# A two-layer network behind linear attention: where the weight products lie in SBUF, when chunk 2 does the next chunk's norm, and when raw weights are stored

## The chip, the cores and the metric

The kernel runs on one core of one Trainium2 chip. The metric is the device time of one execution in microseconds; lower is better. TensorE is called PE, its weight loads PEld, VectorE DVE, ScalarE ACT, GpSimd POOL and SyncE SP. SP issues all large DMAs, in order.

## The reference

```python
def _attn_ref(q, k, v, g_norm):                      # 8 batches, 8 heads, 576 tokens, 64 per head
    kv = np.einsum('bhsd,bhse->bhde', k, v)
    out = np.einsum('bhsd,bhde->bhse', q, kv)
    rms = np.sqrt(np.mean(out * out, axis=-1, keepdims=True) + 1e-06)
    return out / rms * g_norm
def _moe_ref(x, w_in, w_out):                        # x: 4608 x 512, w_in: 512 x 2048, w_out: 2048 x 512
    h = x @ w_in
    g = 0.5 * h * (1.0 + erf(h * np.float32(1.0 / np.sqrt(2.0))))
    return g @ w_out
```

`x` is the attention's output, one row of 512 for each of 4608 tokens. All is float32.

## The kernel before

**Tiling.** The tokens go in nine chunks `c` of 512. Each float32 operand of a large product is kept as two float32r parts, hi and lo, and a product is three matmuls: hi with hi, lo with hi, hi with lo. Chunks 0 and 1 multiply plainly, 16 blocks of the hidden layer one after the other, with matmuls 512 wide (`layer1`, L669, and `layer2`, L696), while the weights are converted and combined. From chunk 2 (`PLAIN`) on, the first layer takes seven products instead of eight for each 2 x 2 block of the matrices: a *pair* `j` (0 to 7) is two blocks of the hidden layer, its products `k` (0 to 6) are six matmuls 256 wide each (`product`, L537), 42 a pair. From chunk 3 (`FAST`) on the second layer does the same in 28 *ticks* `(k, n)` of twelve matmuls (`Fast.matmuls`, L1154). Chunk 2 is the bridge: pairs in the first layer, plain blocks in the second.

**Operands.** In `product` a combination of weights is the stationary operand and `x` the moving one; in `Fast.matmuls` the weights are moving and the activations stationary. The combined weights lie in DRAM (`products`), 512 KB for two of them, and are fetched by SP into a ring of six tiles (`RINGS`; `fetch`, L501): when the last matmul of a tile's content is issued, the content six places on is fetched. Four contents of the first layer stay in w_out4 to w_out7 (`KEPT_IN`, `keep`, L521), seven of the second in `KEPT_OUT`.

**Places.** A tile is 4096 bytes a partition, and the tiles lie in the order of `PLACES`, so all of them begin at the same residue modulo 256 bytes, but for what `EXTRA` adds. `LINE` is 16 floats, 64 bytes. A ring tile has 256 bytes more, in which a fetched content is moved on by `away`: 64 bytes for the first layer, 192 for the second. `KEPT_IN` lies 64 bytes on, `KEPT_OUT` 192 (w_out8 to w_out11, w_in13 to w_in15), and all behind them at residue 0 again. The tiles of `x` and of the activations lie at residue 0. The kv tiles of the attention lie 64 bytes below these, modulo 256. PE's order of matmuls comes from the program as written.

**The next chunk's attention in chunk 2.** Between the two halves of a pair's products, and behind it, `ahead`, `ahead_matmuls` and `ahead_loads` issue the work of chunk 3: `project` (PE, L243), `squares` (ACT, then a sum on DVE), `fold` (PE, L275), `rsqrt` (nine small operations on DVE, L290 to L308), `scale` (a transpose, L320, and a product, L316, on DVE for each of four parts), `add_blocks` (L357) and the split into hi and lo (ACT L362, DVE or POOL L367). `split_kv` (L193, L194) is for chunk 4.

**Weights of the second layer in chunk 2.** By the table `SUMS`, `sum_out` makes the sums of w_out's blocks on POOL (L528: two of 128 x 512, four of 128 x 256), `split_out` splits them on ACT and DVE (L1213, L1214), and `send` in the middle of the next pair has SP store them (L406). Names of buffers for this come from the list `free`. `raw_out` stores blocks that need no sum.

**What waits for what.** Every engine takes its instructions in the order written. A pair's copy on DVE (L553) reads the first product out of its PSUM bank; product 4 adds to that bank, so PE waits for the copy, and for all that stands ahead of it on DVE:

```python
        between[0]()
        product(at, j, 0, a[:, left], True)
        product(at, j, 1, a[:, right])
        nc.vector.tensor_copy(out=p1, in_=a[:, left])
        add(v, a[:, right], p1)
...
        product(at, j, 4, a[:, left])
```

Of the kernel before, what the change touches and what calls it, by code (L numbers as in the profile page):

```python
# [23 lines left out]
FAST = 3  # L24
# [13 lines left out]
def linear_attn_rms_gelu_ffn(  # L38
# [55 lines left out]
    IN_AWAY, OUT_AWAY = LINE, 3 * LINE  # L94
# [398 lines left out]
    def fetch(n):  # L493

        if n < len(queue):
            key = queue[n][1]
            i = RING[n % len(RING)]
            reused(i, F32R)
            away = IN_AWAY if key[0] == "in" else OUT_AWAY
            t = ring[n] = kept[i][:, away:away + 2 * DM]  # L500
            nc.sync.dma_start(out=t.bitcast(F32), in_=products[key])  # L501

    def operand(c, key):
        at = c, key
        return ring[place[at]] if at in place else resident[key]
# [24 lines left out]
    def product(at, j, k, out, first=False):  # L530
        *key, n = place_in(j, k)
        key = tuple(key)
        w, x = operand(at.c, key)[:, n * DM:(n + 1) * DM], at.x[k]
# [457 lines left out]
    def later(c, i):  # L991

        if i < NJ2 - 2:
            raw_out(i)
# [100 lines left out]
    class Fast:  # L1095
# [44 lines left out]
        def matmuls(self, i):  # L1140
# [7 lines left out]
            for p in range(2):  # L1148
                hi, lo = (op[:, z * CH + p * HALF:z * CH + (p + 1) * HALF] for z in range(2))
                wh, wl = (w[:, p * DM + m * HALF:p * DM + (m + 1) * HALF] for m in range(2))  # L1150
# [70 lines left out]
    def send():  # L1221

        for x in sent:
            if isinstance(x, str):
                free.append(x)
# [4 lines left out]
    def ahead(c, j, place):  # L1230
# [34 lines left out]
    def ahead_matmuls(c, j, between):  # L1265
        if c + 1 < NCH:
            for p in {(0, 0): (0,), (1, 0): (1,), (1, 1): (2,), (2, 0): (3,)}.get((j, between), ()):
                attn[c + 1].project(p)
            if (j, between) == (3, 0):
# [70 lines left out]
    SUMS = {0: (0,), 1: (1,), 2: (2, 3), 3: (4,), 4: (5, 6), 7: (7,)}  # L1340
    for c in range(PLAIN, FAST):
        for j in range(NJ2):
# [13 lines left out]
            for n in SUMS.get(j - 1, ()):  # L1356
                split_out(n)
# [98 lines left out]
```

## Time and profile before

| What | Value |
|---|---|
| median of 3 runs | 818.79 us (817.54 to 818.96) |
| the profiled execution | 817.35 us, span 815.5 us |
| PE, PEld busy | 797.0 us, 744.9 us |
| DVE, ACT, POOL busy | 566.2, 369.6, 202.9 us |
| mean granted PE clock | 0.994 |
| HBM read and written | 205.52 and 35.13 MB |

Chunks 0 and 1 end near 213 us, chunk 2 near 313, and a later chunk takes 78 to 90 us by the stages. In the timeline's rows a number ahead of an engine's name is a start and a length in us, `xN` stands for N instructions in a row, and brackets give the idle time of the engine before it and what ended it. A matmul's length overlaps that of the next, so the pace is read from start to start.

### The profile page before, as it was taken

The page shows a single profiled execution, that of the slowest core. Times are in us where ns is not written, and L with a number is a line of the kernel's source. Part 1 is how long each engine was busy: PE and PEld are TensorE (multiplying, and loading weights), DVE is VectorE, ACT ScalarE, POOL GpSimd, SP SyncE. Part 2 cuts the span into 40 slices and gives each one's busy share as a digit, 9 for nine tenths or more (in the row PEclk, how much of TensorE's full clock was granted, in tenths as well). Part 3 has the DMA queues.
Part 4 walks back from the last instruction along what each step waited for, and adds up shares of the span by engine and source line. Part 5 has one row for each costly group of instructions (what it writes and reads, how often), then busy time and mean ns, then how long its engine had stood idle before and what let it go on. Part 6 is the DMA issues. An engine that isn't in the chain of part 4 may idle for free.

```text
span 815.5 us, 16193 instructions
## 1 busy us (share of the span) xinstructions
PE 797.0 (98%) x6248; PEld 744.9 (91%) x6248; DVE 566.2 (69%) x1030; ACT 369.6 (45%) x702; POOL 202.9 (25%) x183
## 2 busy tenths in 40 slices
PE   8999999999997889999999999999999999999998
PEld 6688887888997779999999999999999999999998
DVE  3999756679457673779567865787479748965683
ACT  3788533434452242536254635353445443532361
POOL 1000021102349322380029002710163016201200
PEclk9999999999999799999999999999999999999999
DMA  9981328996797599999999998999889988999884
GB/s 352 409 348 52 117 64 285 362 334 222 295 364 238 196 364 335 393 376 338 348 313 354 326 357 303 361 304 315 307 310 319 324 307 306 291 326 340 315 303 162
DMA packets 90513, 245.39 MB, mean 301 GB/s; under 512 B 9029, under 2 KB 30789, under 8 KB 90437
## 3 DMA queue, kind: packets, MB, share of 16 engines
q1 hardware_dynamic: 90432, 244.35, 84.0%
q8 instruction: 50, 0.82, 0.4%
q14 instruction: 27, 0.21, 0.1%
q10 hardware_dynamic: 4, 0.00, 0.0%
HBM read 205.52 MB, written 35.13 MB: 295 GB/s over the span
## 4 chain that ended last, share of the span: by engine, by line
PE 92%; DMA 3%; DVE 3%; ACT 1%; issue 0%; DVEq 0%; SPq 0%; ACTq 0%
PE acc L1154 20%; PE acc L537 18%; PE h L537 14%; PE acc L696 14%; PE h L669 10%; PE a L1154 8%; PE a L243 3%; PE a L182 2%; DMA w_out<-kv_main 1%; PE h L661 1%; DMA products_out<-w_out 1%; DMA out<-z 1%; DVE w_out L1214 1%; DMA w_in<-products_in 1%; DVE t L299 0%
## 5 line engine op out<-in xcount | busy, mean ns | idle before, releaser
L696 PE MATMUL acc<-w_out,gh 128*128 128x512 f32 x312 | 97.5, 393 | 0.0
L669 PE MATMUL h<-x,w_in 128*128 128x512 f32 x360 | 87.4, 392 | 0.0
L230 POOL TENSOR_TENSOR ql<-q,qh 128x512 fp32r<-128x512 f32 x16 | 21.2, 1327 | 255.3 <-ACT qh L229 255.3
L1154 PE MATMUL acc<-w_in,w_out 128*128 128x256 f32 x660 | 82.7, 279 | 0.0
L669 PEld LDWEIGHTS h<-x,w_in 128*128 128x128 f32 x360 | 67.5, 188 | 14.6 <-POOL x L333 0.2
L1154 PEld LDWEIGHTS acc<-w_in,w_out 128*128 128x128 f32 x660 | 79.2, 188 | 0.0
L537 PE MATMUL acc<-w_out,w_in 128*128 128x256 f32 x540 | 74.4, 280 | 0.0
L696 PEld LDWEIGHTS acc<-w_out,gh 128*128 128x128 f32 x312 | 57.9, 188 | 12.2
L537 PEld LDWEIGHTS acc<-w_out,w_in 128*128 128x128 f32 x540 | 67.5, 188 | 0.3
L696 PE MATMUL acc<-w_out,gl 128*128 128x512 f32 x156 | 61.2, 393 | 1.8 <-DVE gl L688 1.8
L682 ACT ACTIVATE gh<-h 128x512 fp32r<-128x512 f32 x39 | 23.2, 595 | 75.0 <-PE h L669 55.2
L537 PE MATMUL h<-w_in,w_in 128*128 128x256 f32 x348 | 47.2, 287 | 9.7 <-DVE w_in L528 9.7
L537 PEld LDWEIGHTS h<-w_in,w_in 128*128 128x128 f32 x348 | 44.1, 196 | 10.3 <-DVE w_in L528 10.3
L537 PE MATMUL acc<-x,w_in 128*128 128x256 f32 x360 | 48.6, 280 | 0.0
L688 DVE TENSOR_TENSOR gl<-h,gh 128x512 fp32r<-128x512 f32 x39 | 26.8, 686 | 28.9 <-ACT h L683 24.4
L1154 PE MATMUL acc<-w_in,x 128*128 128x256 f32 x360 | 45.8, 279 | 0.0
L537 PEld LDWEIGHTS acc<-x,w_in 128*128 128x128 f32 x360 | 44.7, 188 | 0.3
L537 PE MATMUL h<-w_out,w_in 128*128 128x256 f32 x324 | 44.6, 279 | 0.0
L1154 PEld LDWEIGHTS acc<-w_in,x 128*128 128x128 f32 x360 | 43.5, 188 | 0.0
L537 PE MATMUL h<-x,w_in 128*128 128x256 f32 x312 | 41.6, 280 | 0.5 <-PE acc L696 0.5
L528 DVE TENSOR_TENSOR gl<-acc,gh 128x256 f32<-128x256 f32 (+1 forms) x66 | 29.2, 442 | 18.3 <-ACT gh L574 14.6
L537 PEld LDWEIGHTS h<-w_out,w_in 128*128 128x128 f32 x324 | 40.7, 189 | 0.1
(288 smaller groups left out, 1800.3 us busy)
## 6 DMA issues: line engine op xcount, KB each, us to landing
w_in<-products_in SPq DMA_DIRECT2D x172, 512.0 KB, 5.3
w_in<-products_out SPq DMA_DIRECT2D x126, 512.0 KB, 5.2
kv_main<-kv_main SPq DMA_DIRECT2D x22, 512.0 KB, 6.1
products_in<-w_in SPq DMA_DIRECT2D x40, 256.0 KB, 4.9
w_in<-w_in SPq DMA_DIRECT2D x16, 512.0 KB, 10.2
w_out<-w_out SPq DMA_DIRECT2D x16, 512.0 KB, 10.0
q<-qT SPq DMA_DIRECT2D x15, 512.0 KB, 6.7
products_out<-w_out SPq DMA_DIRECT2D x30, 256.0 KB, 5.3
```

The lines of the kernel that those rows point to most:

```text
L182: nc.tensor.matmul(out=ps[r, n * D:(n + 1) * D], lhsT=k[:, r], rhs=v[:, r], start=(j == 0), stop=(j == NJ),)
L230: eng.tensor_tensor(out=ql, in0=q, in1=qh.bitcast(F32), op=ALU.subtract)
L243: nc.tensor.matmul(out=ps[:, a:e], lhsT=w, rhs=x[:, a:e], start=(m == 0), stop=(m == 2))
L528: eng.tensor_tensor(out=out, in0=x, in1=y, op=op)
L537: nc.tensor.matmul(out=out, lhsT=y, rhs=x[:, z, kb], start=first and kb + i == 0, stop=kb == 1 and i == 2, skip_group_check=True,)
L661: nc.tensor.matmul(out=h, lhsT=ws[i].bitcast(F32)[:, p * P:(p + 1) * P], rhs=at.o_all[:, p], start=(p == 0), stop=(p == NP - 1),)
L669: nc.tensor.matmul(out=h, lhsT=parts["in", i][:, w][:, p * P:(p + 1) * P], rhs=at.x[p][:, x], start=(m + p == 0), stop=(m == 2 and p == NP ...
L682: nc.scalar.activation(out=gh, in_=h, func=AF.Gelu)
L688: nc.vector.tensor_tensor(out=gl, in0=h, in1=gh.bitcast(F32), op=ALU.subtract)
L696: nc.tensor.matmul(out=ps, lhsT=x[:, ts], rhs=parts["out", i][:, w], start=(i == 0 and m == 0), stop=(m == 2 and (i == NF - 1 or (i, t) == ...
L1154: nc.tensor.matmul(out=ps[:, a * HALF:(a + 1) * HALF], lhsT=x[:, at], rhs=y, start=(k in (0, 2, 1) and n + p + a + m == 0), stop=(n == GRO ...
L1214: nc.vector.tensor_tensor(out=t[:, :, 1], in0=s[:, h], in1=t[:, :, 0].bitcast(F32), op=ALU.subtract)
```

## The change

It has four parts. (1) Places: contents of the first layer are moved on by 192 bytes like those of the second, but the first content of each pair has its first product at 0 and its second at 192, in two DMAs of 256 KB instead of one of 512; the second layer's first content (tick 0) lies at 0. `KEPT_IN` is now 192 bytes on. (2) Chunk 2: projections, squares, fold, `rsqrt` and scaling each come one slot sooner, the first scaling's product on POOL. (3) `SUMS` takes one sum behind each of pairs 0 to 3 and 5, two behind pair 4; sum 5's halves go to w_out4 and w_out5, so that w_out6 and w_out7 are loaded first by `keep`. (4) `raw_out` runs two slots later in chunk 1, and its last two calls move from the start of chunk 3 into pairs 1 and 3.

```diff
-    IN_AWAY, OUT_AWAY = LINE, 3 * LINE
+    AWAY = 3 * LINE
...
-    EXTRA[RINGS[-1]] += IN_AWAY
-    EXTRA[KEPT_IN[-1]] = OUT_AWAY - IN_AWAY
-    EXTRA[KEPT_OUT[-1]] = 4 * LINE - OUT_AWAY
+    EXTRA[RINGS[-1]] += AWAY
+    EXTRA[KEPT_OUT[-1]] = 4 * LINE - AWAY
...
-            away = IN_AWAY if key[0] == "in" else OUT_AWAY
-            t = ring[n] = kept[i][:, away:away + 2 * DM]
-            nc.sync.dma_start(out=t.bitcast(F32), in_=products[key])
+            away = [0 if key == ("out", *TICKS[0]) else AWAY] * 2
+            if key == ("in", key[1], 0):
+                away[0] = 0
+            ring[n] = [kept[i][:, a * DM + away[a]:(a + 1) * DM + away[a]] for a in range(2)]
+            if away[0] == away[1]:
+                to = kept[i][:, away[0]:away[0] + 2 * DM]
+                nc.sync.dma_start(out=to.bitcast(F32), in_=products[key])
+            else:
+                for a in range(2):
+                    src = products[key][:, a * DM:(a + 1) * DM]
+                    nc.sync.dma_start(out=ring[n][a].bitcast(F32), in_=src)
...
     def later(c, i):
-        if i < NJ2 - 2:
-            raw_out(i)
+        if 2 <= i < NJ2:
+            raw_out(i - 2)
...
-    def split_out(j):
+    def split_out(j, places=()):
...
-            slot, t = take(F32R)
+            if places:
+                slot, t = places[h], block_tile(places[h], F32R)[:, :2 * DM]
+            else:
+                slot, t = take(F32R)
...
-            if at in ((0, 2), (1, 2), (2, 0), (2, 2)):
-                nxt.squares({(0, 2): 0, (1, 2): 1, (2, 0): 2, (2, 2): 3}[at])
-            if at in ((1, 0), (2, 0)):
-                nxt.split_q(j + 1)
-            if at == (3, 2):
+            for p in {(0, 2): (0,), (1, 0): (1,), (1, 2): (2,), (2, 0): (3,)}.get(at, ()):
+                nxt.squares(p)
+            if at == (0, 2):
+                nxt.split_q(2)
+                nxt.split_q(3)
+            if at == (2, 2):
                 nxt.inv = nxt.rsqrt(sums.pop(c))
-            if at in ((4, 0), (4, 2), (5, 0), (5, 2)):
-                nxt.scale(2 * (j - 4) + place // 2)
-            for k in {(5, 2): ("T3",), (6, 0): ("T1", "T2"), (6, 2): ("T4",)}.get(at, ()):
+            if at in ((3, 2), (4, 0), (4, 2)):
+                nxt.scale(2 * (j - 3) + place // 2)
+            for k in {(5, 0): ("T3",), (5, 2): ("T1", "T2"), (6, 0): ("T4",)}.get(at, ()):
...
-    SUMS = {0: (0,), 1: (1,), 2: (2, 3), 3: (4,), 4: (5, 6), 7: (7,)}
+    SUMS = {0: (0,), 1: (1,), 2: (2,), 3: (3,), 4: (4, 5), 5: (6,), 7: (7,)}
...
-                split_out(n)
+                split_out(n, KEPT_IN[:2] if n == 5 else ())
+            if j == 3:
+                attn[c + 1].scale(0, nc.gpsimd)
...
-            if j > 3:
-                keep(RESIDENT[j - 4])
+            if 4 <= j:
+                keep(RESIDENT[(j - 2) % 4])
...
-                    for n in (NJ2 - 2, NJ2 - 1):
-                        raw_out(n)
                     send()
-                    free.extend(f"w_out{n}" for n in range(NF - 4, NF))
...
+            if c == FAST and second and j in (1, 3):
+                raw_out(NJ2 - 2 + j // 2)
+                free.extend(f"w_out{n}" for n in (NF - 5 + j, NF - 4 + j))
```

Line numbers of the changed kernel are up to 12 higher behind this (L528 is L537 there, L537 is L546, L553 is L562, L1154 is L1163, L1214 is L1226) and one lower ahead of it (L290 is L289, L299 is L298, L320 is L319). How the instructions stand on DVE in chunk 2, from the splits behind pair 3 to the copy of pair 4, before:

```order
L1214 TENSOR_TENSOR w_out_2710<-x_2588,w_out_2710 128x2x256
L290 TENSOR_SCALAR m<-a_2721 128x64
L293 TENSOR_SCALAR y<-m 128x64
L299 SCALAR_TENSOR_TENSOR t<-y 128x64
L304 TENSOR_TENSOR t<-t,m 128x64
L299 SCALAR_TENSOR_TENSOR t<-t 128x64
L299 SCALAR_TENSOR_TENSOR y<-t,y 128x64
L299 SCALAR_TENSOR_TENSOR t<-y 128x64
L308 TENSOR_TENSOR t<-t,m 128x64
L299 SCALAR_TENSOR_TENSOR y<-t,y 128x64
L194 TENSOR_TENSOR kv_l_70<-a_2723,kv_h_68 64x4x64 x2
L320 STREAM_TRANSPOSE sq<-y 128x512
```

And at the same place now, from the splits behind pair 3 to that copy (L562):

```order
L1226 TENSOR_TENSOR w_in_2713<-x_2596,w_in_2713 128x2x256
L1226 TENSOR_TENSOR x_2716<-x_2596,x_2716 128x2x256
L319 STREAM_TRANSPOSE sq<-y 128x512 x2
L315 TENSOR_TENSOR o<-o,sq 128x512
L193 TENSOR_TENSOR kv_l_70<-a_2730,kv_h_68 64x4x64 x2
L319 STREAM_TRANSPOSE sq<-y 128x512
L315 TENSOR_TENSOR o<-o,sq 128x512
L562 COPY w_in_2244<-h_2802 128x256
```

The nine operations of rsqrt are gone from here and three transposes have come. They stand one pair earlier, between the splits behind pair 2 and the copy of pair 3:

```order
L1226 TENSOR_TENSOR x_2589<-x_2449,x_2589 128x2x256
L1226 TENSOR_TENSOR w_out_2592<-x_2449,w_out_2592 128x2x256
L289 TENSOR_SCALAR m<-a_2603 128x64
L292 TENSOR_SCALAR y<-m 128x64
L298 SCALAR_TENSOR_TENSOR t<-y 128x64
L303 TENSOR_TENSOR t<-t,m 128x64
L298 SCALAR_TENSOR_TENSOR t<-t 128x64
L298 SCALAR_TENSOR_TENSOR y<-t,y 128x64
L298 SCALAR_TENSOR_TENSOR t<-y 128x64
L307 TENSOR_TENSOR t<-t,m 128x64
L298 SCALAR_TENSOR_TENSOR y<-t,y 128x64
L562 COPY w_in_2244<-h_2643 128x256
```

Before, one sum over `part` (L266) stood there. On POOL, the sums behind pair 2, before (two whole sums, six rows each, the last of the first and all of the second):

```order
L528 TENSOR_TENSOR x_2580<-w_out_2579,x_2580 128x256
L528 TENSOR_TENSOR w_in_2587<-w_out_717 128x512
L528 TENSOR_TENSOR w_in_2587<-w_out_771 128x512
L528 TENSOR_TENSOR x_2588<-w_in_2587 128x256
L528 TENSOR_TENSOR x_2588<-x_2588,w_in_2587 128x256
L528 TENSOR_TENSOR x_2588<-w_in_2587 128x256
L528 TENSOR_TENSOR x_2588<-w_in_2587,x_2588 128x256
L230 TENSOR_TENSOR ql<-q,qh 128x512
```

And now:

```order
L537 TENSOR_TENSOR x_2596<-w_out_2595,x_2596 128x256
L229 TENSOR_TENSOR ql<-q,qh 128x512
L315 TENSOR_TENSOR o<-o,sq 128x512
L537 TENSOR_TENSOR w_out_2722<-w_out_717 128x512
L537 TENSOR_TENSOR w_out_2722<-w_out_771 128x512
```

The second sum now comes behind pair 3, after the split of chunk 4's q and the first scaling's product. On SP, a first content of a pair in chunk 2, with the fetch ahead of it, before and now:

```order
L501 DMA w_in_2238<-products_in_3_1781 128x1024
L501 DMA w_in_1509<-products_in_0_1769 128x1024
L406 DMA products_out_0_2532<-x_2573 128x512
L406 DMA products_out_0_2534<-x_2573 128x512
L406 DMA products_out_0_2536<-w_out_2576 128x512
```

```order
L504 DMA w_in_2240<-products_in_3_1778 128x1024
L508 DMA w_in_1500<-products_in_0_1766 128x512 x2
L405 DMA products_out_0_2548<-x_2589 128x512
L405 DMA products_out_0_2550<-x_2589 128x512
L405 DMA products_out_0_2552<-w_out_2592 128x512
```

One DMA has become two. The order of PE's matmuls changes only where projections and fold stand.

More of the change, by code (lines that the diff above doesn't have):

```diff
@@ L532, in product @@
         key = tuple(key)
-        w, x = operand(at.c, key)[:, n * DM:(n + 1) * DM], at.x[k]
+        w, x = operand(at.c, key)[n], at.x[k]
         for kb in range(2):
@@ L1149, in matmuls @@
                 hi, lo = (op[:, z * CH + p * HALF:z * CH + (p + 1) * HALF] for z in range(2))
-                wh, wl = (w[:, p * DM + m * HALF:p * DM + (m + 1) * HALF] for m in range(2))
+                wh, wl = (w[p][:, m * HALF:(m + 1) * HALF] for m in range(2))
                 for a in range(2):
@@ L1224, in send @@
             if isinstance(x, str):
-                free.append(x)
+                if x not in KEPT_IN:
+                    free.append(x)
             else:
@@ L1266, in ahead_matmuls @@
         if c + 1 < NCH:
-            for p in {(0, 0): (0,), (1, 0): (1,), (1, 1): (2,), (2, 0): (3,)}.get((j, between), ()):
+            for p in {(0, 0): (0,), (0, 1): (1,), (1, 0): (2,), (1, 1): (3,)}.get((j, between), ()):
                 attn[c + 1].project(p)
-            if (j, between) == (3, 0):
+            if (j, between) == (2, 0):
                 sums[c] = attn[c + 1].fold()
```

4 lines of the change are left out of this document (3 added, 1 removed).

## The prediction

> **What bounds the kernel now.** I read the page first, then busy time by stage, then who waited for whom, then the timeline.
>
> ```profile
> span 815.5 us, 16193 instructions
> PE 797.0 (98%) x6248; PEld 744.9 (91%) x6248; DVE 566.2 (69%) x1030; ACT 369.6 (45%) x702; POOL 202.9 (25%) x183
> ```
>
> TensorE is busy for 797.0 of 815.5 us. So only two things can be saved: the 18.5 us in which it idles, and the pace at which it takes its matmuls, since no matmul is removed. By stage (columns: window, length, PE, PEld, DVE, ACT, POOL busy and counts, granted clock, DMA share, GB/s):
>
> ```profile
> 258.00:279.00 21.00, 13.52 (x70) 12.04 (x69) 15.86 (x27) 4.21 (x8) 13.49 (x17) 0.76 0.59 201
> 263.60:273.90 10.30, 5.82 (x23) 5.43 (x24) 6.09 (x14) 1.58 (x4) 8.15 (x10) 0.50 0.79 295
> ...
> 313.00:403.00 90.00, 90.00 (x805) 88.55 (x804) 61.56 (x112) 41.05 (x79) 24.65 (x18) 1.00 0.96 357
> ```
>
> Chunk 3 (third row) and the later ones have no PE gap and a full clock. Chunk 2 (213 to 313 us) has a hole of 7.48 us (first row), and in and behind it 10.3 us at half the clock (second row). The next rows are that hole, on DVE, POOL and PE:
>
> ```profile
> 252.66 1.29 DVE L1214 TENSOR_TENSOR w_out<-x,w_out 128x512 fp32r<-128x512 f32 x1
> ...
> 256.78 0.21 DVE L290 TENSOR_SCALAR m<-a 128x64 f32<-128x64 f32 x1
> 257.69 1.55 PE L537 MATMUL h<-x,w_in 128*128 128x256 f32 x12
> 258.08 0.74 POOL L528 TENSOR_TENSOR w_out<-x 128x256 f32<-128x256 f32 x1
> ...
> 261.10 2.48 POOL L528 TENSOR_TENSOR x<-w_out 128x512 f32<-128x512 f32 x2
> ...
> 263.69 0.77 DVE L299 SCALAR_TENSOR_TENSOR y<-t,y 128x64 f32<-128x64 f32 x1
> 267.15 0.42 DVE L553 COPY w_in<-h 128x256 f32<-128x256 f32 x1
> 268.08 4.21 PE L537 MATMUL h<-w_in,w_in 128*128 128x256 f32 x18 [7.48 <-DVE w_in L528]
> ```
>
> The nine operations of rsqrt take from 256.78 to 264.46, 7.68 us, while POOL runs the sums of output weights without a pause. In a later chunk, with POOL not in the way, the same nine take from 340.21 to 342.47, 2.26 us:
>
> ```profile
> 340.21 0.21 DVE L290 TENSOR_SCALAR m<-a 128x64 f32<-128x64 f32 x1
> 342.25 0.22 DVE L299 SCALAR_TENSOR_TENSOR y<-t,y 128x64 f32<-128x64 f32 x1
> ```
>
> So POOL beside it costs (7.68 - 2.26) / 9 = 0.60 us for each operation. Pair 4's copy (L553) stands behind them on DVE and starts at 267.15, and PE cannot start product 4 before. Of the stretch at half clock PE worked 5.82 us, so it lost another 2.9. Smaller gaps follow in pairs 6 and 7:
>
> ```profile
> 293.32 2.32 PE L537 MATMUL h<-w_in,w_in 128*128 128x256 f32 x18 [1.58 <-DVE w_in L528]
> 299.20 0.62 ACT L362 CAST w_out<-w 128x512 fp32r<-128x512 f32 x1 [5.84 <-DMA products_out<-w_out]
> 301.63 1.65 PE L537 MATMUL h<-x,w_in 128*128 128x256 f32 x12 [0.52 <-PE acc L696]
> 305.36 0.86 PE L537 MATMUL h<-w_in,w_in 128*128 128x256 f32 x5 [0.66 <-DVE w_in L528]
> ```
>
> Chunk 2 thus idles 7.48 + 1.58 + 0.52 + 0.66 = 10.24 us, 13.1 with the clock. The ACT row is behind the last two: a cast in the queue ahead of the gelu waited 5.84 us for a store to leave its buffer.
>
> **The pace of the matmuls.** The matmuls 256 wide (all of L537 and L1154) run at two paces, for tens of us at a time:
>
> ```profile
> 385.85 2.99 PE L1154 MATMUL a<-w_in,x 128*128 128x256 f32 x24
> 388.67 1.58 PE L1154 MATMUL a<-w_in,w_in 128*128 128x256 f32 x12
> ...
> 701.13 1.52 PE L1154 MATMUL acc<-w_in,w_out 128*128 128x256 f32 x12
> 702.49 1.52 PE L1154 MATMUL acc<-w_in,x 128*128 128x256 f32 x12
> ```
>
> 24 in 2.82 us is 117.5 ns from start to start; 12 in 1.36 us is 113.3. Over longer stretches the starts lie 117.8 ns apart (the long step) and 113.3 (the short step), so a long one costs 4.45 ns. The same code does both, so a step is entered and then kept. Busy time and count of L1154 in a layer 2 with the long step and one with the short, and of L537 in the longest stretch of long steps in layer 1:
>
> ```profile
> 450.00:486.00 36.00, 36.00 (x308) 36.00 (x307) 1.00 0.95 338
> 697.00:732.00 35.00, 35.00 (x311) 35.00 (x311) 1.00 0.91 311
> ...
> 735.00:772.00 37.00, 37.00 (x316) 37.00 (x316) 1.00 0.92 328
> ```
>
> Layer 2 has the long step in chunks 3, 4 and 5 and the short one in 6, 7 and 8: 3 x 336 long, 4.5 us. Layer 1 has about 1190 long of 2352, in nine stretches: 5.3 us.
>
> What sets the step? Call distance the residue of the stationary operand's place less that of the moving one, modulo 256 bytes. It is 64 in layer 1 (weights stationary, 64 on) and 64 in layer 2 (weights moving, 192 on, so -192). Chunk 1 has 512 wide matmuls at other distances, since w_out4 to 7 lie 64 on and w_out8 to 11 lie 192 on:
>
> ```profile
> 150.20 0.63 PE L696 MATMUL acc<-w_out,gh 128*128 128x512 f32 x2
> ...
> 152.96 0.40 PE L669 MATMUL h<-x,w_in 128*128 128x512 f32 x1
> ...
> 179.82 0.63 PE L696 MATMUL acc<-w_out,gh 128*128 128x512 f32 x2
> ...
> 182.62 2.90 PE L669 MATMUL h<-x,w_in 128*128 128x512 f32 x12
> 185.36 0.63 PE L696 MATMUL acc<-w_out,gh 128*128 128x512 f32 x2
> ```
>
> Twelve at distance 192 take 2.76 us (150.20 to 152.96), twelve at 64 take 2.80 (179.82 to 182.62), and the twelve at distance 0 right behind take 2.74, coming back to the short step within a few matmuls. Equal residues lead out of the long step. At 192 the nearest 256 wide rows are the projections L243, whose kv tiles lie 64 bytes below q's modulo 256:
>
> ```profile
> 326.28 0.28 PE L243 MATMUL a<-qh,kv_h 128*128 128x256 f32 x1
> ...
> 327.69 0.84 PE L537 MATMUL acc<-w_out,w_in 128*128 128x256 f32 x6
> ...
> 332.45 0.28 PE L243 MATMUL a<-qh,kv_h 128*128 128x256 f32 x1
> ...
> 333.81 0.39 PE L537 MATMUL h<-w_out,w_in 128*128 128x256 f32 x2
> ```
>
> Twelve behind long steps take 1.41 us, twelve behind short ones 1.36: distance 192 keeps the step it finds.
>
> The Trainium skill (TensorE: Matmul & The Clock Gate, Step-by-step: what each phase is for) says that TensorE has two independent read ports on SBUF, so that loading the next weights takes nothing from the running matmul; by this rule the places cannot matter, no pace changes, and the sum below would be 808.7 instead of 799.5. The 2.80 against 2.74 us above, at the same shape, speak against it.
>
> **The change part by part.** *Places.* Each pair of layer 1 now begins with six matmuls at distance 0, then 36 at 192; layer 2 begins with twelve at 0 and goes on at 64, where the short step can hold (697 to 732). If six are enough to reach it, or it is never left, 5.3 + 4.5 = 9.8 us go. The bounds are the long step in all of layer 1 (1160 more, +5.2 us) and in none of it. I take 9.5, since pairs behind interrupted work begin with a few long ones. w_out4 to 7 now lie 192 on, so layer 2 of chunks 0 and 1 pays 0.04 us per slot there: 8 slots, +0.3 us.
>
> *Split loads.* A pair's first weights arrive as two DMAs of 256 KB, 8 more issues a chunk on SP; TensorE reads the first half first, so only the second half comes one issue later. Cover: a ring slot is fetched five slots of 12 matmuls ahead, 5 x 1.36 = 6.8 us, against a landing of 5.3:
>
> ```profile
> w_in<-products_in SPq DMA_DIRECT2D x172, 512.0 KB, 5.3
> ```
>
> I cost it at nothing (0 to 0.3 us a pair if the cover fails).
>
> *The norm one slot sooner.* rsqrt goes from behind pair 3 to behind pair 2, where DVE had an idle 2.63 us, but POOL's four subtractions lie there:
>
> ```profile
> 242.20 0.68 DVE L1214 TENSOR_TENSOR w_out<-x,w_out 128x512 fp32r<-128x512 f32 x1
> 243.65 0.74 POOL L528 TENSOR_TENSOR x<-w_out 128x256 f32<-128x256 f32 x1 [5.87 <-DMA products_out<-x]
> 246.14 0.42 DVE L553 COPY w_in<-h 128x256 f32<-128x256 f32 x1 [2.63 <-PE h L537]
> ```
>
> From 242.9, 2.26 us end at 245.1; with six of nine held up, 3.6 more, 248.7. PE released the copy at 246.14, behind product 1, and wants it done twelve matmuls later, at 247.5, before product 4; ending at 249.1 it is 1.6 late, by the short end not at all. I take 0.9. Behind pair 3 DVE now has two splits instead of four, two transposes with POOL's multiply (1.3) between them, one product, kv_l (1.3) and another transpose and product: 1.4 + 0.7 + 1.3 + 0.7 + 0.7 + 1.3 + 1.4 = 7.5 us from 252.66, and with the copy 260.6; pair 4, begun at 257.69, wants it done 24 matmuls on, at 260.4: 0.2 late, and 2.0 with POOL in the way of three, 1.0 taken. Pair 5 by the same count 0 to 1.3, 0.6 taken. Pair 6 has 1.4 us less on DVE ahead of its copy: 0.2 to 1.4 left, 0.5 taken. The sums now go one, one, one, two, one per pair and sum 5's halves use w_out4 and w_out5, so the cast of 299.20 takes a buffer that POOL has left: 0 (to 1.2). Together 3.0 us, from 0.2 to 7.7, all too short for the clock by the 1.58 us row, which kept it. Gain: 13.1 - 3.0 = 10.1, between 5.4 and 12.9.
>
> *Stores spread.* SP's raw stores move two slots on in chunk 1 and into pairs 1 and 3 of chunk 3. No PE wait lies there: 0.
>
> **Sum.** The profiled execution took 817.35 us (span 815.5), 1.4 below the median of 818.79. 818.8 - 10.1 - 9.5 + 0.3 = 799.5.
>
> **Rivals.** *Paces stay a matter of chance* (places do nothing that lasts): 818.8 - 10.1 = 808.7. For it: at distance 64 both steps last. Against it: the twelve at distance 0. Chance 0.16. The Trainium skill's rule on two ports (same page and section) ends at the same place. *Distance 192 holds layer 1 at the long step*, six matmuls being too few: 818.8 - 10.1 - 4.5 + 5.2 + 0.3 = 809.7. For it: twelve L243 kept the long step, and twelve 512 wide ones at 192 took 2.76 us, at 0 only 2.74. Chance 0.12. *The hole only moves*: rsqrt meets POOL behind pair 2 as it did behind pair 3, another wait of 7 us and a lower clock: the paces alone are left, 818.8 - 9.5 + 0.3 = 809.6. Against it: POOL has only four operations there. Chance 0.06. *Slower*: the second half of a pair's first weights lands late. In 56 pairs of seven chunks it decides from 19.3 / 56 = 0.34 us a pair, one more issue on SP if every fetch had no slack; then 819 and more. Against it: no row shows PE waiting on a DMA there. Chance 0.04. The forecast itself: 0.62.
>
> What a measurement can tell from no change is about 0.2%, 1.6 us. Faster 0.94, same 0.02, slower 0.04. The range runs from 794 (all of 12.9 and 9.8 saved, with the run at the low end) to 810, which takes in the first three rivals.
>
> **What would show it.** In the changed profile: L290 to L299's nine operations start near 243 and no PE gap in chunk 2 exceeds 2 us, with the clock at 1.00 from 258 to 279; L1154 and L537 show a mean of 276 ns, not 281, in every chunk, and L537 at 281 would mean the second rival. PE waiting on a DMA at a pair's second product would be the last. The forecast falls if layer 1 stays mixed, or if rsqrt still takes 7 us.

## The result and the profile after

The changed kernel takes 809.87 us (median of 4 runs, 808.53 to 809.99) against 818.70 for the kernel before on the same chip: ratio 0.9891, 95% interval 0.9874 to 0.9908. It is 8.8 us faster where 19.3 were forecast. The profiled execution took 808.53 us; its page begins:

```profile
span 806.7 us, 16291 instructions
PE 793.6 (98%) x6248; PEld 741.2 (92%) x6248; DVE 564.7 (70%) x1029; ACT 369.4 (46%) x702; POOL 207.7 (26%) x184
```

PE is busy for 3.4 us less and idle for 5.4 less. By the first matmul of each stage in the two traces (us; the last column is the best kernel of the experiments, `combined`, below):

| Stage | before | after | combined |
|---|---|---|---|
| up to chunk 2 | 212.9 | 211.3 | 211.6 |
| chunk 2 and layer 1 of chunk 3 | 150.3 | 147.2 | 143.4 |
| layer 2, chunks 3, 4, 5 | 39.7, 39.6, 39.6 | 38.2, 38.2, 38.2 | 38.2, 38.4, 38.3 |
| layer 2, chunks 6, 7, 8 | 38.1, 38.1, 38.0 | 38.2, 38.2, 38.1 | 38.2, 38.2, 38.1 |
| layer 1, chunks 4, 5, 6 | 44.5, 45.1, 43.4 | 45.5, 45.8, 43.1 | 44.8, 45.1, 42.7 |
| layer 1, chunks 7, 8 | 42.6, 39.6 | 42.1, 38.6 | 41.1, 38.1 |

So 1.6 us came from chunks 0 and 1, 3.1 from chunk 2 and the layer behind it (chunk 2 itself went from 100.1 to 95.9 us, layer 1 of chunk 3 from 50.2 to 51.3), 4.0 from layer 2, and 0.1 from layer 1 of chunks 4 to 8: 8.7 in the trace. The waits of PE in chunk 2, from the timeline, and from the windows the stretch behind the last of them:

```profile
246.95 2.31 PE L546 MATMUL h<-w_in,w_in 128*128 128x256 f32 x18 [0.86 <-DVE w_in L537]
261.12 2.39 PE L546 MATMUL h<-w_in,w_in 128*128 128x256 f32 x18 [0.75 <-DVE w_in L537]
272.90 2.31 PE L546 MATMUL h<-w_in,w_in 128*128 128x256 f32 x18 [1.09 <-DVE w_in L537]
287.56 3.84 PE L546 MATMUL h<-w_in,w_in 128*128 128x256 f32 x18 [3.93 <-DVE w_in L537]
```

```profile
287.90:291.50 3.60, 3.60 (x19) 3.60 (x18) 1.03 (x3) 0.88 (x2) 0.00 (x0) 0.53 1.06 406
```

The hole of 7.48 us in pair 4 is gone. Pairs 3, 4 and 5 wait 0.86, 0.75 and 1.09 us; pair 6 waits 3.93 us, and 3.6 us behind it run at 0.53 of the clock, a loss of 3.6 x 0.47 = 1.7. On DVE and POOL ahead of that wait:

```profile
279.09 3.53 DVE L1226 TENSOR_TENSOR w_out<-x,w_out 128x512 fp32r<-128x512 f32 x3
282.54 1.77 DVE L356 TENSOR_TENSOR o<-o 128x512 f32<-128x512 f32 x1
284.23 1.75 DVE L356 TENSOR_TENSOR w<-z,o 128x512 f32<-128x512 f32 x1
286.02 0.69 DVE L356 TENSOR_TENSOR z<-o,w 128x512 f32<-128x512 f32 x1
286.63 0.42 DVE L562 COPY w_in<-h 128x256 f32<-128x256 f32 x1
...
280.88 1.19 POOL L537 TENSOR_TENSOR w_out<-w_out,w_out 128x256 f32<-128x256 f32 x1
282.02 3.41 POOL L366 TENSOR_TENSOR x<-o,x 128x512 fp32r<-128x512 f32 x2
```

The copy that PE waits for starts at 286.63, behind four splits of sums (L1226, three of them shown) and the sums of blocks T1, T2 and T4 (L356). T1 and T2 stood ahead of this copy before, too; T4 is new there, while a scaling and T3 have left. Before, from the first of the four splits to the copy, with POOL idle for 19.36 us up to the last row:

```profile
286.59 1.28 DVE L1214 TENSOR_TENSOR w_out<-x,w_out 128x512 fp32r<-128x512 f32 x2
...
291.79 0.68 DVE L357 TENSOR_TENSOR w<-z,o 128x512 f32<-128x512 f32 x1
292.39 0.42 DVE L553 COPY w_in<-h 128x256 f32<-128x256 f32 x1
292.40 2.98 POOL L367 TENSOR_TENSOR x<-o,x 128x512 fp32r<-128x512 f32 x2 [19.36 <-ACT x L362]
```

DVE took 5.80 us for this before and takes 8.26 now (278.37 to 286.63), for fewer operations, because POOL works beside it: on sums up to 282.07, then on the splits of two blocks (L366) up to 285.43. The third L356, with POOL done, takes 0.69 us, the two beside POOL 1.77 and 1.75. The Trainium skill (SBUF — State Buffer, Who interferes with whom) says that a VectorE instruction with two SBUF inputs and a GpSimd one that reads SBUF shut each other out for a whole instruction; these rows agree with it.

For the paces, a layer 2 from its first matmul, and the busy time and count in the stretch of chunk 4 that had the long step before:

```profile
687.76 1.60 PE L1163 MATMUL acc<-w_in,w_out 128*128 128x256 f32 x12
689.20 1.54 PE L1163 MATMUL acc<-w_in,x 128*128 128x256 f32 x12
690.58 1.52 PE L1163 MATMUL acc<-w_in,w_out 128*128 128x256 f32 x12
691.94 1.52 PE L1163 MATMUL acc<-w_in,x 128*128 128x256 f32 x12
```

```profile
443.00:479.00 36.00, 36.00 (x319) 36.00 (x318) 29.15 (x49) 19.53 (x37) 1.02 (x1) 1.00 0.97 341
```

The twelve of tick 0, at distance 0, take 1.44 us: 120 ns each, more than the long step. The next tick takes 1.38 us, and from there on a tick takes 1.36, 113.3 ns a matmul. 319 matmuls in 36 us now stand where 308 stood before. Layer 1 is still mixed: of its 2016 matmuls at distance 192 46% have the short step; the 336 at distance 0 lie mostly 116 to 121 ns apart.

### The profile page after: what moved, and what is told of

It is laid out like the page before. It is cut to its first block, busy times and chain, and to the rows that moved or that the text cites. A ratio compares the mean times of both kernels' runs of the same rounds, so it can differ in the third digit from the quotient of the medians.

```text
span 806.7 us, 16291 instructions
## 1 busy us (share of the span) xinstructions
PE 793.6 (98%) x6248; PEld 741.2 (92%) x6248; DVE 564.7 (70%) x1029; ACT 369.4 (46%) x702; POOL 207.7 (26%) x184
## 4 chain that ended last, share of the span: by engine, by line
PE 89%; DMA 6%; DVE 3%; issue 1%; POOL 0%; SPq 0%; ACT 0%; POOLq 0%
PE acc L1163 20%; PE acc L546 17%; PE acc L705 14%; PE h L546 13%; PE h L678 10%; PE a L1163 8%; PE a L242 3%; DMA w_in<-products_in 2%; PE a L181 2%; DMA kv_tail<-kv_tail 1%; PE h L670 1%; DMA w_out<-kv_main 1%; DMA q<-qT 1%; DMA products_out<-x 1%; DVE w_out L1226 1%
## 5 line engine op out<-in xcount | busy, mean ns | idle before, releaser
L546 PE MATMUL acc<-w_out,w_in 128*128 128x256 f32 x600 | 80.0, 280 | 0.2 <-DMA w_in<-products_in 0.2
L546 PEld LDWEIGHTS acc<-w_out,w_in 128*128 128x128 f32 x600 | 73.9, 188 | 0.6 <-issue 0.4
L1163 PE MATMUL acc<-w_in,w_out 128*128 128x256 f32 x576 | 71.6, 277 | 0.0
L1163 PEld LDWEIGHTS acc<-w_in,w_out 128*128 128x128 f32 x576 | 68.3, 188 | 0.0
L546 PE MATMUL acc<-x,w_in 128*128 128x256 f32 x360 | 49.4, 279 | 0.0
L546 PE MATMUL h<-w_in,w_in 128*128 128x256 f32 x312 | 42.2, 286 | 6.7 <-DVE w_in L537 6.6
L1163 PE MATMUL acc<-w_in,x 128*128 128x256 f32 x384 | 48.0, 276 | 0.0
L546 PE MATMUL h<-w_out,w_in 128*128 128x256 f32 x360 | 47.8, 279 | 0.0
L546 PEld LDWEIGHTS h<-w_in,w_in 128*128 128x128 f32 x312 | 39.4, 194 | 7.7 <-DVE w_in L537 7.7
L1163 PEld LDWEIGHTS acc<-w_in,x 128*128 128x128 f32 x384 | 45.7, 188 | 0.0
L546 PEld LDWEIGHTS acc<-x,w_in 128*128 128x128 f32 x360 | 45.1, 188 | 0.2
L546 PEld LDWEIGHTS h<-w_out,w_in 128*128 128x128 f32 x360 | 44.4, 188 | 0.0
L1163 PE MATMUL acc<-w_in,w_in 128*128 128x256 f32 x336 | 42.2, 277 | 0.0
L546 PE MATMUL h<-x,w_in 128*128 128x256 f32 x312 | 42.0, 279 | 0.0
```

Source lines behind the costliest of these rows:

```text
L546: nc.tensor.matmul(out=out, lhsT=y, rhs=x[:, z, kb], start=first and kb + i == 0, stop=kb == 1 and i == 2, skip_group_check=True,)
L1163: nc.tensor.matmul(out=ps[:, a * HALF:(a + 1) * HALF], lhsT=x[:, at], rhs=y, start=(k in (0, 2, 1) and n + p + a + m == 0), stop=(n == GRO ...
```

## The experiments

Times are compared with the kernel before on the same chip, whose median was 817.3, 817.4 and 817.9 us in the three groups, against 818.7 for the result above; so times from different chips can differ by 1.4 us without any change.

**The two parts alone.** The first kernel is the one before with the new places (`AWAY`, `EXTRA`, `fetch` and `operand` as in the change, nothing else). The second is the changed kernel with the old places:

```diff
-            away = [0 if key == ("out", *TICKS[0]) else AWAY] * 2
-            if key == ("in", key[1], 0):
-                away[0] = 0
+            away = [IN_AWAY if key[0] == "in" else OUT_AWAY] * 2
```

> The kernel before with the new places (and split loads) alone; chunk 2, SUMS and the stores as before. Theory (places act through the distance): layer 2 takes the short step in every chunk (3 x 336 x 4.45 ns = 4.5 us less, 72 matmuls at distance 0 cost 0.5), layer 1's 336 matmuls at distance 0 cost 2.2 us, the rest of layer 1 stays mixed: 818.8 - 4.5 + 0.5 + 2.2 = 817.0 us. Rival (the step is a matter of when a stage begins, places do nothing that lasts): 818.8, with layer 2 long in some chunks.

Measured 817.25 us, ratio 1.0007 (0.9988 to 1.0026): nothing. The time is the rival's, the reason is not. In the trace layer 2 of chunks 3 and 5 takes 38.2 us instead of 39.6, as the theory had it; that of chunk 4 leaves the short step in its seventh tick, behind a matmul 0.06 us late, and takes 39.4. But layer 1 of chunk 4 takes 45.5 instead of 44.5, and chunk 2 with layer 1 of chunk 3 takes 153.2 instead of 150.3: pair 4's wait came out longer than before, and PE waited for a load of the ring in chunk 3 (second row; in total, times, longest):

```profile
268.64 3.97 PE L546 MATMUL h<-w_in,w_in 128*128 128x256 f32 x18 [8.35 <-DVE w_in L537]
...
PE h L546 <- DMA w_in<-products_in: 1.4, 1, 1.4
```

The longer wait in pair 4 need not come from the places, for `stores_alone` has 8.19 us there with the old ones. The load came late behind split ones: from 329.6 us on SP issued six contents as eight DMAs in 4.8 us, where the kernel before issued six in 3.4. That the split is the cause was not tried alone.

> The changed kernel with the places of before (layer 1 at 64, layer 2 at 64, one DMA for each load); norm, SUMS and stores as changed. Theory: the chunk-2 part is worth 13.1 - 8.2 = 4.9 us and chunks 0 and 1 another 1.6 (their wait at 120 to 140 us goes with the later stores): 818.8 - 6.5 = 812.3 us, with layer 2 at mixed steps again. Rival (the 1.6 us in chunks 0 and 1 come from the places of w_out4 to w_out7): 813.9. Rival (steps are a matter of timing): layer 2 short in every chunk here too, about 808.

Measured 811.55 us, ratio 0.9923 (0.9899 to 0.9947): 5.7 us by the medians, 6.3 by the ratio, and so the theory's 6.5. Chunk 2 begins at 210.7 us, so the gain in chunks 0 and 1 does not come from the places. Layer 2 takes 39.7, 38.5 and 39.6 us in chunks 3, 4 and 5, so at least in chunks 3 and 5 the short step does come from the places. With both parts the gain is 8.8, with this one 5.7 to 6.3: on top of it the places are worth about 3 us, with some 2 us of doubt, where 9.2 were forecast.

**The stores alone.** The kernel before, with the raw stores moved as in the change and nothing else:

```diff
-        if i < NJ2 - 2:
-            raw_out(i)
+        if 2 <= i < NJ2:
+            raw_out(i - 2)
```

> The kernel before with the raw stores moved (two slots later in chunk 1, the last two into pairs 1 and 3 of chunk 3) and nothing else. Theory (the 1.8 us in which PE waited for gl near 131 us were caused by the stores ahead of it): that wait is gone and chunk 2 starts 1.8 us sooner, 818.8 - 1.8 = 817.0 us. Rival (the prediction's term: they cost and bring nothing, the wait went with the places or with the sums): 818.8.

Measured 814.68 us, ratio 0.9963 (0.9945 to 0.9981), 3.3 us by the medians and so more than the theory, and chunk 2 starts at 210.8 instead of 212.9. The mechanism, in the kernel before on SP, DVE and PE, and then in this one on DVE:

```profile
118.63 1.58 SPq L406 DMA_DIRECT2D products_out<-w_out  x3
120.25 1.15 SPq L738 DMA_DIRECT2D out<-w  x1
...
128.09 0.69 DVE L417 TENSOR_TENSOR z<-w_in 128x512 f32<-128x512 f32 x1 [5.95 <-DMA out<-z]
...
131.76 0.50 PE L696 MATMUL acc<-w_out,gl 128*128 128x512 f32 x1 [1.84 <-DVE gl L688]
```

```profile
126.22 0.69 DVE L417 TENSOR_TENSOR z<-w_in 128x512 f32<-128x512 f32 x1 [4.17 <-DMA out<-z]
```

Three raw stores stood on SP ahead of chunk 0's output. DVE waited for the buffer that this output leaves, gl was late behind it, and PE waited 1.84 us for gl. Without the three stores DVE goes on 1.87 us sooner and PE does not wait. The prediction put the stores at nothing with the words "No PE wait lies there", though the list of PE's waits before had this one. The rest of the 3.3 us lies, in the trace, in chunk 4's layer 2, which happened on the short step part of the way (38.4 us).

**What sets the step.** The changed kernel without the six at distance 0 at the start of a pair:

```diff
-            if key == ("in", key[1], 0):
-                away[0] = 0
```

> The changed kernel without the exception for the first content of a pair: all of layer 1 at distance 192, one DMA for each load; tick 0 of layer 2 stays at 0. Theory A (a step once entered is kept, and layer 2 now ends with the short one): the six at distance 0 go (336 x 6.6 ns = 2.2 us) and layer 1 stays at the short step, some 1000 long ones x 4.45 ns = 4.5 us less: 809.9 - 6.7 = 803.2 us. Theory B (layer 1 is mixed whatever the six do): 809.9 - 2.2 = 807.7. Rival (192 holds the long step): all 2352 long, 809.9 - 2.2 + 5.9 = 813.6.

Measured 807.63 us, ratio 0.9877 (0.9851 to 0.9903): theory B's time to 0.1 us. But its trace shows what the mixture is made of. Chunk 4's layer 1 begins behind a layer 2 at the short step; the second and third lines below lie behind the first projection:

```profile
397.63 2.88 PE L544 MATMUL h<-w_out,w_in 128*128 128x256 f32 x24
400.36 2.88 PE L544 MATMUL acc<-w_out,w_in 128*128 128x256 f32 x24
...
406.65 3.01 PE L544 MATMUL acc<-w_out,w_in 128*128 128x256 f32 x24
409.50 0.87 PE L544 MATMUL acc<-w_in,w_in 128*128 128x256 f32 x6
410.21 0.87 PE L544 MATMUL acc<-w_out,w_in 128*128 128x256 f32 x6
```

24 in 2.73 us up to the projection (113.8 ns), six in 0.71 behind it (118.3). The projections of this chunk are cut at a batch's edge, 320 and 192 wide. In chunks 4, 5 and 6 every matmul from the first such projection to the end of layer 1 is long, but for one part of chunk 5; in chunk 7, whose projections are not cut, and in chunk 8, which has none, every one is short. So a step is kept until other work on PE breaks it (projections with two widths, sum_kv); at 192 such a break nearly always leads to the long one.

Then the twelve of a pair's first content at distance 0, behind such breaks and in every pair of chunk 2 (`at_0` names the pairs):

```diff
-            if key == ("in", key[1], 0):
-                away[0] = 0
+            if key[0] == "in" and key[2] == 0 and (queue[n][0] == PLAIN or at_0(queue[n][0], key[1])):
+                away = [0, 0]
```

> Layer 1 at distance 192 as in layer1_all_192, but both products of a pair's first content (twelve matmuls, one DMA) lie at distance 0 in every pair of chunk 2 and, in later chunks, in the first pair behind each projection, fold or sum_kv: pairs 0, 2 to 5 of chunk 3, 2 to 5 of chunks 4 and 5, 2 to 4 of chunk 6. Theory (twelve at distance 0 always end in the short step, 192 keeps it, and other work between the pairs is what breaks it): behind each such twelve the rest of layer 1 is at 113.3 ns; chunks 3 to 6 give back 0.8 to 1.0 us each, chunk 2 some 0.8 (all against 117.8, with 24 of 2.2 ns more per pair): 807.6 - 4.4 = 803.2 us. Rival (the step is set by something else, as by the load of the memory): as layer1_all_192 with 288 matmuls at 120 instead of 117.8 ns, 808.2 us.

Measured 805.46 us, ratio 0.9849 (0.9821 to 0.9877). The first rows behind chunk 4's first projection:

```profile
403.82 2.97 PE L549 MATMUL acc<-w_out,w_in 128*128 128x256 f32 x24
406.62 0.84 PE L549 MATMUL acc<-w_in,w_in 128*128 128x256 f32 x6
407.30 0.84 PE L549 MATMUL acc<-w_out,w_in 128*128 128x256 f32 x6
```

Twelve at distance 0 and twelve at 192 take 2.80 us, and from there six take 0.68 (113.3 ns), where they took 0.71. This holds behind all the twelves of chunks 3 to 6. The gain on `layer1_all_192` is 2.2 us, half of what was expected. Most of the other half shows in the trace: layer 2 of chunk 4 fell to the long step in its seventh tick, where one matmul came 0.07 us late, and took 39.4 us instead of 38.2, and in chunk 2 the waits behind product 3 broke the step again.

All of both layers at distance 0 is one number:

```diff
-    AWAY = 3 * LINE
+    AWAY = 0
```

> The changed kernel with AWAY = 0: all 256 wide matmuls of both layers at distance 0. Theory (at 256 wide, distance 0 itself costs 120 ns a matmul, and only what follows it at another distance is short): 4368 x 120 = 524.2 us against 502.6 in the changed kernel, 809.9 + 21.6 = 831 us. Rival (the step of the prediction: distance 0 leads to the short step and stays there; the 120 ns are only a passage): 4368 x 113.3 = 494.9, 802 us.

Measured 827.21 us, ratio 1.0110 (1.0075 to 1.0145). A row of layer 2:

```profile
452.68 3.04 PE L1163 MATMUL acc<-w_in,w_out 128*128 128x256 f32 x24
```

The next row starts at 455.56: 24 in 2.88 us, 120.0 ns, and so in all 2010 steps of L1163 from one matmul to the next within a layer 2. Distance 0 is no way into the short step; it is a third pace, 6.7 ns above it. The whole fell 4 us short of the 831 expected. Chunk 2 starts at 209.7 us here, 1.6 sooner than in the changed kernel, and the kernel before is 1.3 us faster on this chip than on the one of the result; the remaining 1 us is not accounted for.

The kv tiles at the residue of q, so that the projections lie at distance 0, on top of `layer1_all_192`:

```diff
-    kv_h = [const.tile([P, NP, P], F32R, name=f"kv_h{s}") for s in range(2)]
-    kv_l = [const.tile([P, NP, P], F32R, name=f"kv_l{s}") for s in range(2)]
...
     for name in PLACES:
         block_tile(name, F32)
+    kv_h = [const.tile([P, NP, P], F32R, name=f"kv_h{s}") for s in range(2)]
+    kv_l = [const.tile([P, NP, P], F32R, name=f"kv_l{s}") for s in range(2)]
```

> layer1_all_192 with the kv tiles placed behind the weights, at the same residue as q: the projections are at distance 0 instead of 192, the rest is unchanged. Theory (the projections break the short step of chunks 4 to 6 because of their distance): layer 1 stays at the short step through the projections of chunks 4, 5 and 6 at least up to sum_kv, 120 to 270 matmuls a chunk, 0.5 to 1.2 us each: 807.6 - 1.5 to 3.3 = 804.3 to 806.1 us. Rival (it is the cut at a batch's edge, two widths in a projection, that breaks it, whatever the distance): 807.6.

Measured 807.88 us, ratio 0.9875 (0.9852 to 0.9897): the rival's time. Chunk 4 goes from 0.68 us for six to 0.71 across the first projection, as at 192:

```profile
403.01 0.84 PE L544 MATMUL h<-w_out,w_in 128*128 128x256 f32 x6
403.69 0.84 PE L544 MATMUL h<-x,w_out 128*128 128x256 f32 x6
...
408.76 0.87 PE L544 MATMUL acc<-w_in,w_in 128*128 128x256 f32 x6
409.47 0.87 PE L544 MATMUL acc<-w_out,w_in 128*128 128x256 f32 x6
```

But the rival's reason does not hold either: in chunk 7, where the projections are not cut, layer 1 is long behind them in this kernel and short in `layer1_all_192`. Cut projections break the step, and projections at distance 0 do so even when they are not cut.

**The hole in pair 6.** The changed kernel with T1, T2 and T4 behind pair 6's copy:

```diff
-            for k in {(5, 0): ("T3",), (5, 2): ("T1", "T2"), (6, 0): ("T4",)}.get(at, ()):
+            for k in {(5, 0): ("T3",), (6, 1): ("T1", "T2"), (6, 2): ("T4",)}.get(at, ()):
```

> The changed kernel with the sums of blocks T1, T2 and T4 behind pair 6's copy instead of ahead of it. Theory (pair 6's wait of 3.93 us is these three operations, 4.2 us on DVE with POOL beside them, and the half clock behind it comes from the wait): the wait falls under 0.5 us and the clock stays at 1.00: 809.9 - 3.5 - 1.6 = 804.8 us. Rival (the wait moves on to pair 7, whose copy then stands behind T4 and the low parts): 808 to 810.

Measured 807.58 us, ratio 0.9878 (0.9852 to 0.9903), near the rival. Pair 6 waits for nothing now. Pair 7 does, and the clock is at 0.50 from 296.5 to 303.4 us; the cast (ACT) ahead of its copy waits for a store of the sums to leave a buffer:

```profile
297.13 4.21 PE L546 MATMUL h<-w_in,w_in 128*128 128x256 f32 x18 [3.12 <-DVE w_in L537]
...
292.85 0.62 ACT L1225 CAST w_out<-w_out 128x512 fp32r<-128x512 f32 x1 [1.16 <-DMA products_out<-w_out]
```

Next, T4 and the low parts of T2 and T4 on POOL, which stands idle there:

```diff
-                nxt.add_blocks(k)
+                nxt.add_blocks(k, nc.gpsimd if at == (6, 2) else nc.vector)
...
-                nxt.low_block(n, nc.vector)
+                nxt.low_block(n, nc.gpsimd if at in ((6, 2), (7, 0)) else nc.vector)
```

> blocks_later with T4 and the low parts of T2 and T4 on POOL instead of DVE: nothing of the blocks stands ahead of pair 7's copy on DVE, only the two splits that wait for stores of the sums. Theory (of pair 7's wait of 3.12 us there, 2.1 are those three operations, and the half clock goes with the wait): wait under 1.2 us, clock at 1.00: 807.6 - 2.0 - 1.6 = 804.0 us. Rival (the stores are what the wait is made of: the splits end only then): the wait stays over 2 us and the time at 806.5 to 807.6.

Measured 808.14 us, ratio 0.9877 (0.9855 to 0.9899). The wait in pair 7 fell to 0.71 and the clock stayed at 1.00 up to 310 us, as the theory had it, and chunk 3's first products start at 302.45 instead of 307.22 us, 4.8 sooner than in the changed kernel. Yet the time is what it was. Layer 2 of chunk 4 fell to the long step in its seventh tick (39.4 us instead of 38.2), and above all the wait has moved on once more, past the end of chunk 2:

```profile
294.74 2.39 PE L546 MATMUL h<-w_in,w_in 128*128 128x256 f32 x18 [0.71 <-DVE w_in L537]
312.94 0.98 PE L546 MATMUL acc<-w_in,w_in 128*128 128x256 f32 x6 [2.07 <-DVE w L744]
...
304.73 2.54 POOL L537 TENSOR_TENSOR x<-w_out 128x512 f32<-128x512 f32 x2 [7.05 <-DMA w_out<-w_out]
...
310.99 1.29 DVE L1226 TENSOR_TENSOR x<-w_out,x 128x512 fp32r<-128x512 f32 x2 [5.16 <-DMA q<-qT]
312.20 1.28 DVE L744 COPY w<-acc 128x512 f32<-128x512 f32 x2
```

Sum 7 on POOL waits 7.05 us for the DMA that empties its buffer and starts at 304.73, as it does in `blocks_later` (304.60). Its split on DVE starts at 310.99, behind ACT's cast of the sum (the bracket names a load of q, which ended last by the profile); the copies out of the acc banks (L744) stand behind that, and PE waits for them. The 2.07 us and the 3.4 us at half clock that follow (314.5 to 317.9, 1.7 us lost) eat 3.8 of the 4.8. PE comes to chunk 3 4.8 us sooner, but that DMA only 1.4 (sum 7 starts at 306.14 in the changed kernel). The remedy is to put the split behind the copies:

```diff
-                    split_out(NJ2 - 1)
                     second_layer(*sorted(g))
                     store(acc.pop(c - 1), (c - 1) * CH)
+                    split_out(NJ2 - 1)
```

> blocks_on_pool with sum 7's split put behind the store of chunk 2's output at the start of chunk 3, so that the copies out of the acc banks (L744) no longer stand behind that split on DVE. Theory (the hole of pair 6 was worth 5 us but came back as a wait of 2.07 us on L744 with the half clock behind it, about 1 us more; sum 7 waits on POOL for the DMA that empties its buffer, whatever comes before): 808.1 - 3.1 = 805.0 us, no PE wait over 0.5 us between 300 and 320 us. Rival (the split is late for the next pair's sums on DVE instead): a wait of 1 to 2 us within 8 us behind, 807 to 808.

Measured 805.05 us, ratio 0.9845 (0.9806 to 0.9885): the theory. No PE wait over 0.5 us is left between 300 and 320 us. Columns as in the prediction's windows; the same stretch of the changed kernel and of this one:

```profile
213.00:320.00 107.00, 100.35 (x696) 90.61 (x696) 70.29 (x126) 40.97 (x77) 52.64 (x51) 0.98 0.88 310
```

```profile
213.00:320.00 107.00, 102.89 (x729) 93.10 (x728) 70.83 (x126) 44.04 (x83) 56.80 (x54) 1.00 0.90 317
```

PE starts 33 matmuls more in it, and the clock is 1.00. Layer 2 of chunk 4 is on the long step in part here too (39.4 us). This is the gain that the prediction had booked under the norm; it needed three moves more.

**Both parts.** `combined` is `store_first` with the edit of `twelve_behind_breaks`, and tick 8 of chunk 4 at distance 0 too:

```diff
+            if queue[n] == (4, ("out", *TICKS[8])):
+                away = [0, 0]
```

> store_first with layer 1 at 192 and the twelve at distance 0 behind breaks (as in twelve_behind_breaks); in chunk 4 the content of tick 8 lies at distance 0 too, behind the place where PE waits 0.1 us for a load and layer 2 may fall to the long step. Theory (the two parts add): 805.0 - 4.4 (809.9 to 805.5 for the twelve) - 0 to 1.0 = 799.6 to 800.6 us. Rival (the steps depend on all that comes before, so the parts don't add): 802 to 804.

Measured 802.11 us (801.25 to 802.76), ratio 0.9811 (0.9775 to 0.9846), the fastest of all, 1.5 us above the theory and at the lower end of the rival's 802 to 804: the parts do not quite add. The two windows are of the changed kernel and of this one, from 320 us on:

```profile
320.00:803.00 483.00, 482.65 (x4329) 480.30 (x4328) 339.55 (x620) 218.33 (x421) 128.69 (x94) 1.00 0.92 324
```

```profile
320.00:803.00 483.00, 475.23 (x4298) 472.83 (x4296) 339.51 (x616) 215.99 (x417) 128.77 (x94) 1.00 0.91 323
```

Its own span ends at 800.1. From its list of waits (in total, times, longest):

```profile
PE h L551 <- DVE w_in L542: 4.4, 4, 1.5
PE acc L551 <- DMA w_in<-products_in: 0.9, 1, 0.9
```

With fewer long steps PE catches up with the ring at one place, in layer 1 of chunk 3, and waits 0.9 us for a load, where the changed kernel waited 0.2. That is about half of the 1.5 us.

The last kernel is `combined` with layer 1 at 64 and fewer twelves:

```diff
-            away = [0 if key == ("out", *TICKS[0]) else AWAY] * 2
+            away = [IN_AWAY if key[0] == "in" else 0 if key == ("out", *TICKS[0]) else OUT_AWAY] * 2
...
+        return j in {2: (0, 1, 2, 3, 6, 7), 6: (0, 3)}.get(c, (0,))
```

> As combined, but layer 1 at distance 64 as before, with twelve at distance 0 only in the first pair of a chunk, in pairs 1, 2, 3, 6 and 7 of chunk 2 and pair 3 of chunk 6. Theory (at 64 a break leads to the short step, as behind L182 and L243 before, at 192 to the long one; only the passage from layer 2 needs the twelve): some 156 matmuls at 120 and nearly all others of layer 1 at 113.3 ns, 267.5 us against 273.6: 805.0 - 6.1 - 0 to 1.0 = 797.9 to 798.9 us. Rival (distance 64 and 192 are alike, and the break decides): long stretches behind L182 and L243 as at 192, 802 to 804.

Measured 803.71 us, ratio 0.9827 (0.9784 to 0.9869): the rival's time, but not its reason. The half of the theory that speaks of breaks held: behind the first projection of chunk 4 (second and third row) six take 0.68 us, where at 192 they took 0.71. The other half fell: behind the twelve at distance 0 that open the chunk six take 0.71 (first row, and the next starts at 398.92):

```profile
398.21 0.87 PE L552 MATMUL h<-w_in,w_in 128*128 128x256 f32 x6
...
404.61 0.84 PE L552 MATMUL acc<-w_in,w_in 128*128 128x256 f32 x6
405.29 0.84 PE L552 MATMUL acc<-w_out,w_in 128*128 128x256 f32 x6
```

So it is not the twelve alone that lead to the short step, but the way out of them: weights moved on by 192 bytes (layer 1 at 192; layer 2, where they are the moving operand) lead to the short step, weights moved on by 64 to the long one.

## Why the prediction was wrong

Of the 19.3 us forecast 8.8 came. By the stages chunk 2 brought 5.9 less than its term and the paces 6.5 less, the stores 1.6 more, and the 0.3 for w_out4 to w_out7 does not show apart from these.

- **Chunk 2, 10.1 us forecast, 4.8 measured** by waits and clock (13.1 - 6.6 - 1.7), 4.2 by the length of the stage. Right: rsqrt near 242, its last four operations slowed by POOL to 0.66 to 0.79 us, waits of 0.86, 0.75 and 1.09 us in pairs 3 to 5 (0.9, 1.0, 0.6 taken), pair 7 free. The term that failed is pair 6, "0.2 to 1.4 left, 0.5 taken": it measured 3.93, and 1.7 more by the clock. The count set what left DVE ahead of that copy against what came, at durations without POOL; but POOL now runs sums 4, 5 and 6 and then the splits of two blocks there without a break, and beside it three splits on DVE took 3.53 us and two block sums 1.76 each. `blocks_later`, `blocks_on_pool` and `store_first` show that the loss is real and can be had back, by way of two more waits that stood behind it. "All too short for the clock" failed with it. (By its own terms the bounds of what is left, 0.2 to 7.7 us, should read 0.4 to 7.5; nothing hangs on that.)
- **Paces, 9.5 us forecast, 4.0 measured in layer 2, while layer 1 lost about 1** (1.1 more in chunk 3, 0.1 less in chunks 4 to 8). The step that failed is "Equal residues lead out of the long step". It was read from twelve matmuls 512 wide. At 256 wide distance 0 is the dearest place (120.0 ns in `all_at_0`), so 336 matmuls of layer 1 and 72 of layer 2 lost up to 6.7 ns each against the short step: 2.7 us, for which the sum had no term. For layer 2 the conclusion held in the changed kernel, where all six chunks run short; but that is in part luck, since in `places_alone`, `twelve_behind_breaks`, `blocks_on_pool` and `store_first`, with the same places in layer 2, chunk 4 falls back (39.4 us). For layer 1 the condition "if six are enough" did not.
- **The rivals.** The times of the second (809.7) and third (809.6) are the nearest to 809.9, and both by luck. The second kept the norm's 10.1 us, of which 4.8 at most came, and had layer 1 lose 5.2, of which 1 came; 192 does not hold the long step (chunks 7 and 8 of `layer1_all_192` are short throughout), but the breaks at 192 mostly lead into it. The third was right that the hole moves, but it moved to pair 6 and not to pair 3, and it counted the paces at 9.5. The first rival's reason, that places do nothing lasting, is refuted by layer 2 and by `all_at_0`. Nor does the conclusion hold that the prediction drew from the rule on PE's two read ports (the Trainium skill, TensorE: Matmul & The Clock Gate, Step-by-step: what each phase is for): with only places changed, the same matmuls took 113.3 to 120.0 ns. Whether the ports have to do with it no run shows.
- **Stores, 0 forecast, 1.6 to 2.1 us measured** (`stores_alone`). A wait of 1.8 us that was there in the profile was not followed to its cause.
- **w_out4 to w_out7 at 192, +0.3 us forecast**: chunk 2 starts at 210.7 to 211.2 us in the three kernels with the new stores and w_out4 to w_out7 at 64, at 211.0 to 211.8 with them at 192, and at 212.7 against 212.9 for the places alone. The term is within this scatter and stays open.
- **Split loads, 0**: PE waited 0.2 us for a load of the ring in the whole kernel. Right here; in `places_alone` it waited 1.44 us for one, so the cover is thin.

## What to carry to other kernels

Price an operation that is moved by its duration beside what runs on the other engines at the new place, and follow the queue behind it to the next wait, and the next; here one hole moved three times before it was gone. A pace read at one width is no evidence for another: try the place itself, at the width that matters, before building a sum on it. A wait that the page lists is followed to its DMA queue before a move of stores is put at nothing.

## What the runs showed of the hardware

- The pace of matmuls 256 wide depends on where the two operands lie, modulo 256 bytes: 120.0 ns with both at one residue, and elsewhere 113.3 or 117.8 ns, either of which lasts for hundreds of matmuls until other work breaks it. Which of the two follows a break depends on the place (at 64 mostly the short, at 192 mostly the long); behind twelve at one residue it is the short with weights 192 bytes on, and the long with 64. In layer 2, also at 64, a matmul of chunk 4 that came 0.04 to 0.07 us late led to the long step in four kernels, and one 0.02 to 0.08 us late did not in three others. Why is not known.
- The record of the granted clock in the traces has only 1.00 and 0.50, and it changes on a grid of 3.41 us: but for the one at the very end of a kernel, a drop lasts 3.41, 6.83 or 10.24 us. Cut along this grid, in the fourteen traces, every stretch at 1.00 in which PE idled for 55% or more of the time is followed by 0.50, and none with 49% or less is; at 0.50, 18% idle or more kept it there, and 8% or less ended it. So the place of a wait counts beside its length. Waits of 1.84 and 1.58 us (kernel before) left the clock at 1.00. The 2.07 us of `blocks_on_pool`, 1.9 of them in one stretch, led to 3.41 us at 0.50, the 3.12 us of `blocks_later` to 6.83, and the 3.93 of the changed kernel to 3.41. The Trainium skill (TensorE: Matmul & The Clock Gate, What's actually happening) puts the drop behind an idle window of about 3.4 us; the grid here has that length, but a stretch idle for a little over half of it was enough.
